# Regrouping the attention of a four-layer transformer kernel: two bursts per period in place of three

## The chip, the cores and the metric

The kernel runs on one core of a Trainium2 chip. The metric is the device time of one execution in microseconds (us). The engines of the core run side by side: TensorE (PE in the profile, its weight loads are PEld), VectorE (DVE), ScalarE (ACT), GpSimd (POOL), and SyncE (SP), which here only issues transfers. TensorE writes its results to PSUM, which this kernel uses as eight banks of 128 x 512 numbers in f32; ACT and DVE read a bank and so make it free again.

## The reference

The input `x` has 2048 rows of 640. Four layers are added to it in turn, A, B, A, B, each on a layer norm of what is there. Both kinds have 32 heads of width 20.

```python
# A: linear attention
pq, pk = phi(q), phi(k)
kv  = einsum("bhsd,bhse->bhde", pk, v);  z = einsum("bhsd->bhd", pk)
o   = (pq @ kv) / (pq @ z + 1e-6)                 # then @ wo
# B: four segments of 512 rows, with a memory over the segments before
logits = q_s @ k_s.T * scale + causal_mask        # 512 x 512 for each head
a_dot  = softmax(logits) @ v_s
a_mem  = (phi(q_s) @ M) / (phi(q_s) @ z + 1e-6)
o      = g * a_mem + (1 - g) * a_dot              # then @ wo
M, z   = M + phi(k_s).T @ v_s, z + sum(phi(k_s))
```

The change concerns `a_dot` alone.

## The kernel before

Two streams of instructions are made and merged. The **dense** stream makes projections, memories, transposes and output products of all layers; its large parts are the lines 388 (a product of 15 matmuls of 320 columns) and 374 (15 matmuls of 512 columns). The **attention** stream makes `a_dot` of the two B layers. `Kernel.run` takes from the stream whose planned cost so far is smaller. TensorE's order is exactly the order in which the code is written (`MANUAL = ("PE",)`). The other engines' instructions are ordered by a scheduler.

Attention goes by groups of four heads: eight groups in a segment, four segments, two B layers, so 64 groups. Of a group, the heads are named by `p` and `par` (0 or 1 each). Keys and queries of `par` 0 lie in rows 0 to 63 and those of `par` 1 in rows 64 to 127, and the matmuls of two `par` run beside each other on the two halves of TensorE. Blocks of 128 rows of a segment are counted by `i` (queries) and `j` (keys); only blocks with j <= i are computed, so a row of blocks has 512, 384, 256 or 128 columns. A group needs these steps:

- `max`, `row_max`, line 999 on TensorE: scores with a query block stationary, five parts (`MAXES`) of two PSUM banks each; DVE takes the maximum of each row in line 1006. `split` (lines 1015 and 1016) and `rows` (a transpose on TensorE in line 1024, a copy on ACT in line 1026, two transfers on SP) put the negative maxima as extra rows into the query stack `qs`.
- `exp`, `scores`, line 1041 on TensorE: scores with a key block stationary, with the maxima subtracted, five parts (`EXPS`) of two banks. ACT takes the exponential of each bank (line 1045, result `pe`), and POOL sets the blocks on the diagonal to zero above it (line 1052, a select). Parts 0 and 1 hold the key block j = 0; part 2 the blocks j = 1 and 3 of `p` = 0; part 3 the same of `p` = 1; part 4 the block j = 2 of all four heads.
- `sum`, `weigh`, line 1068 on TensorE: the four heads' exponentials times the values of block j, on four column groups at once, in f32, into one bank `pv`. So `sum` 1 and `sum` 3 need `exp` 2 and 3, and `sum` 2 needs `exp` 4.
- `copy` (ACT, line 1074) empties `pv`; `out` (line 1081, four transposes on TensorE, then DVE lines 1084 and 1091 and an addition on POOL or DVE) normalizes.

The order of these steps is written out by hand in `STRETCHES`. Each entry names the step, its part, and how many periods back the group is that it works on (0 the newest group, 2 the oldest). One pass over all stretches is a period. All that one stretch issues follows on TensorE without dense work in between (a burst). After a stretch the attention stream yields `SLOT`, the planned cost of the dense work that is let in behind it, in ns.

PSUM banks come from one pool with eight buffers, shared by both streams:

```python
def bank(self):
    return self.ps.tile([P, 512], F32, tag="ps", name="ps", bufs=8)
```

Of the kernel before, what the change touches and what calls it, by code (L numbers as in the profile page):

```python
# [39 lines left out]
VW = H * E1 + 11  # L40
HB = H // 2
COL = 1 / 2.4
SLOT = 2420.0
R_SECOND, R_PROJ, R_MID, R_END = 2.2, 1.0, 1.2, 0.85


# [5 lines left out]
EXPS += [[((0, a, 2, 0), (1, a, 2, 256)) for a in range(2)]]  # L52


STRETCHES = [[("exp", 4, 2), ("max", 0, 0), ("max", 1, 0), ("sum", 0, 2), ("rows", 0, 1), ("sum", 1, 2), ("sum", 3, 2),
              ("sum", 2, 2), ("copy", 0, 2), ("max", 2, 0)],
             [("out", 0, 2), ("exp", 0, 1), ("exp", 1, 1), ("max", 3, 0)],
             [("exp", 2, 1), ("exp", 3, 1), ("max", 4, 0), ("split", 0, 0), ("load", 0, 0)]]


def constants():
# [69 lines left out]
class Kernel:  # L131
# [965 lines left out]
    def attention(self, segs):  # L1097
# [3 lines left out]
        while n < NSEG * NG or prev or old:  # L1101
# [7 lines left out]
            n += 1  # L1109
            for stretch in STRETCHES:  # L1110
                for op, k, back in stretch:
# [18 lines left out]
                    elif op == "out":  # L1130
                        if not G["st"].get("remembered"):
                            yield lambda: G["st"].get("remembered")
                        self.normalize(G)
                yield SLOT
            old, prev = prev, new
# [192 lines left out]
```

## Time and profile before

| what | value |
|---|---|
| median of 3 runs | 1765.23 us (1764.43 to 1766.04) |
| the profiled execution | 1769.35 us, its span 1767.6 us |
| TensorE busy | 1683.3 us, 95% of the span |
| DVE, ACT, POOL busy | 1195.1, 971.2 and 517.4 us |
| mean granted TensorE clock | 0.992 |

The profile is of one execution. A busy TensorE counts each matmul from its start to a modelled end, and matmuls overlap by about 0.17 us, so short stalls are partly hidden in the busy time; distances from start to start tell more. Attention of the first B layer lies between about 350 and 953 us of the span, that of the second between about 1214 and 1743 us.

### The profile page before, as it was taken

The page shows a single profiled execution, that of the slowest core. Times are in us where ns is not written, and L with a number is a line of the kernel's source. Part 1 is how long each engine was busy: PE and PEld are TensorE (multiplying, and loading weights), DVE is VectorE, ACT ScalarE, POOL GpSimd, SP SyncE. Part 2 cuts the span into 40 slices and gives each one's busy share as a digit, 9 for nine tenths or more (in the row PEclk, how much of TensorE's full clock was granted, in tenths as well). Part 3 has the DMA queues.
Part 4 walks back from the last instruction along what each step waited for, and adds up shares of the span by engine and source line. Part 5 has one row for each costly group of instructions (what it writes and reads, how often), then busy time and mean ns, then how long its engine had stood idle before and what let it go on. Part 6 is the DMA issues. An engine that isn't in the chain of part 4 may idle for free.

```text
span 1767.6 us, 36360 instructions
## 1 busy us (share of the span) xinstructions
PE 1683.3 (95%) x13032; PEld 1050.2 (59%) x13032; DVE 1195.1 (68%) x3856; ACT 971.2 (55%) x1818; POOL 517.4 (29%) x982
## 2 busy tenths in 40 slices
PE   5989999999999999999989999999999999999998
PEld 4666667564565576456556777566546545644555
DVE  7554434487787677658864465846888877878773
ACT  5454443347656645567666453333675576666664
POOL 1533441012123312333342211221421432233452
PEclk9999999999999999999999999999999999999999
DMA  6432343422322322353211303433232323223432
GB/s 245 155 133 105 142 167 110 154 71 72 109 84 67 110 96 80 113 161 99 80 42 39 113 31 120 157 107 121 69 102 83 109 80 105 93 84 107 130 110 90
DMA packets 118333, 187.61 MB, mean 106 GB/s; under 512 B 13948, under 2 KB 79612, under 8 KB 115848
## 3 DMA queue, kind: packets, MB, share of 16 engines
q1 hardware_dynamic: 105896, 142.68, 25.5%
q0 software_dynamic: 3040, 21.63, 3.4%
q10 hardware_dynamic: 9216, 20.98, 3.1%
q8 instruction: 103, 1.69, 0.4%
q14 instruction: 78, 0.64, 0.1%
HBM read 106.05 MB, written 78.64 MB: 104 GB/s over the span
## 4 chain that ended last, share of the span: by engine, by line
PE 73%; DVE 12%; ACT 6%; issue 3%; DMA 3%; POOL 2%; SPq 0%; ACTq 0%; DVEq 0%; POOLq 0%
PE ps L388 31%; PE ps L374 15%; PE ps L1068 6%; DVE junk L1006 4%; PE ps L1041 3%; PE ps L313 3%; PE ps L999 3%; ACT pe L1045 3%; PE ps L557 3%; PE ps L443 3%; PE ps L884 1%; PE ps L1081 1%; PE ps L723 1%; DMA qs<-mt 1%; DVE st L331 1%
## 5 line engine op out<-in xcount | busy, mean ns | idle before, releaser
L1006 DVE CUSTOM_DVE_ANT_0 junk<-ps,maskw 128x512 bf16<-128x512 f32 (+3 forms) x1024 | 499.4, 488 | 94.3 <-PE ps L999 34.0
L1045 ACT ACTIVATE pe<-ps,lsc 128x512 f32<-128x512 f32 x640 | 394.7, 695 | 100.4 <-PE ps L1041 97.1
L1052 POOL TENSOR_SCALAR_AFFINE_SELECT pe<-pe 128x256 f32<-128x256 f32 (+1 forms) x640 | 229.6, 365 | 453.6 <-ACT pe L1045 449.3
L388 PEld LDWEIGHTS <-xT 128*128 128x128 f16 x2880 | 281.7, 99 | 115.7 <-issue 9.7
L388 PEld LDWEIGHTS <-oT 128*128 128x128 f16 x1920 | 186.5, 99 | 82.6 <-issue 7.5
L1068 PE MATMUL ps<-pe,v 128*32 128x512 f32 (+3 forms) x2048 | 161.5, 439 | 7.7 <-POOL pe L1052 3.4
L388 PE MATMUL ps<-w_Bo,oT 128*128 128x320 f16 x960 | 144.5, 304 | 2.3 <-ACT oT L317 1.2
L374 PE MATMUL ps<-xT,w_Bq 128*128 128x512 f16 x600 | 142.1, 383 | 1.7 <-ACT pe L1045 0.8
L388 PE MATMUL ps<-w_Bv,xT 128*128 128x320 f16 x960 | 140.7, 301 | 0.7 <-ACT v L421 0.7
L999 PE MATMUL ps<-ks,qs 60*128 60x384 f16 (+3 forms) x1024 | 128.8, 298 | 12.5 <-DVE mg L1006 3.6
L374 PE MATMUL ps<-xT,w_Bk 128*128 128x512 f16 x600 | 138.8, 379 | 1.0 <-DVE mg L1006 0.5
L388 PE MATMUL ps<-w_Ak,xT 128*128 128x320 f16 x960 | 137.3, 300 | 0.6 <-ACT r L402 0.5
L1041 PE MATMUL ps<-qs,ks 62*128 62x512 f16 (+3 forms) x1024 | 107.4, 301 | 5.4 <-DMA qs<-mt 3.7
L414 POOL TENSOR_SCALAR e<-e 128x320 f32<-128x320 f32 (+1 forms) x52 | 82.1, 1578 | 88.7 <-ACT e L410 85.7
L849 DVE SCALAR_TENSOR_TENSOR nat<-ps,nat 128x512 f16<-128x512 f32 x80 | 54.9, 687 | 77.9 <-ACT nat L848 71.2
L1068 PEld LDWEIGHTS ps<-pe,v 128*32 128x32 f32 x2048 | 63.7, 110 | 65.3 <-issue 43.8
L848 ACT ACTIVATE nat<-ps 128x512 f16<-128x512 f32 x80 | 48.1, 601 | 94.8 <-PE ps L374 70.9
L999 PEld LDWEIGHTS <-qs 60*128 60x128 f16 x1024 | 51.1, 94 | 82.5 <-issue 55.1
L374 PEld LDWEIGHTS <-w_Bq 128*128 128x128 f16 x600 | 57.1, 98 | 67.0 <-issue 9.8
L374 PEld LDWEIGHTS <-w_Bk 128*128 128x128 f16 x600 | 57.4, 98 | 65.2 <-issue 5.3
L336 POOL TENSOR_TENSOR rs<-rs,mhalf 128x1 f32<-128x1 f32 x48 | 27.0, 564 | 227.0 <-DVE rs L335 214.3
L421 ACT ACTIVATE v<-ps 128x320 f32<-128x320 f32 x96 | 41.7, 436 | 91.5 <-PE ps L388 90.2
(220 smaller groups left out, 2680.3 us busy)
## 6 DMA issues: line engine op xcount, KB each, us to landing
x<-xn ACTq DMA_DIRECT2D x48, 320.0 KB
qs<-qd SPq DMA_DIRECT2D x128, 120.0 KB
ks<-kd SPq DMA_DIRECT2D x128, 120.0 KB
xo<-x SPq DMA_DIRECT2D x48, 320.0 KB
pqi<-pqd SPq DMA_DIRECT2D x32, 320.0 KB
qd<-nat SPq DMA_DIRECT2D x40, 256.0 KB
kd<-nat SPq DMA_DIRECT2D x40, 256.0 KB
x<-in_A_x SPq DMA_DIRECT2D x16, 320.0 KB
```

The costliest lines, as they stand in the source:

```text
L313: nc.tensor.transpose(pt[:, (c - c0) * P:(c - c0 + 1) * P], src[:, c * P:(c + 1) * P], self.ident)
L374: nc.tensor.matmul(p, w[:, c, a, t * P:(t + 1) * P], xT[:, c, b, :], start=k == 0, stop=k == 3 * C - 1)
L388: nc.tensor.matmul(p, xT[:, c, a, i * P:(i + 1) * P], w[:, c, b, n * HN:(n + 1) * HN], start=k == 0, stop=k == 3 * C - 1)
L414: nc.gpsimd.tensor_scalar(e, e, 1.0, eps, op0=OP.min, op1=OP.add)
L443: nc.tensor.matmul(nd[:, lo - k * cut:hi - k * cut], pq[t], mem[:, OFF[t] + lo - a:OFF[t] + hi - a], start=first, stop=True, skip_group_ch ...
L849: nc.vector.scalar_tensor_tensor(nat[:, 1], p, QK_SHIFT, nat[:, 0], op0=OP.mult, op1=OP.subtract)
L999: nc.tensor.matmul(bs[par][:, a:a + n], qs[r, p, i * P:(i + 1) * P], ks[r, p, :n], start=True, stop=True)
L1006: nc.vector.tensor_tensor_reduce(junk[:, :n], bs[par][:, a:a + n], self.maskw[:, SEG - n:], 1.0, NEG, OP.add, OP.max, G["mg"][:, par, p, i ...
L1041: nc.tensor.matmul(b[:, a:a + n], ks[r, p, j * P:(j + 1) * P], qs[r, p, j * P:], start=True, stop=True)
L1045: nc.scalar.activation(e, b, AF.Exp, scale=self.lsc)
L1052: nc.gpsimd.affine_select(d, d, pattern=pat, compare_op=OP.is_ge, fill=0.0, base=0, channel_multiplier=-1)
L1068: nc.tensor.matmul(G["pv"][32 * h4:32 * h4 + 32, j * P:], v[j][:, h * E1:h * E1 + 32], G.pop((p, par, j)), start=j == 0, stop=j == 2, skip ...
```

## The change

The three stretches become two, and `SLOT` grows by half, so that the planned dense work of a period (2 x 3630 against 3 x 2420 ns) stays the same.

```diff
-SLOT = 2420.0
+SLOT = 3630.0
...
-STRETCHES = [[("exp", 4, 2), ("max", 0, 0), ("max", 1, 0), ("sum", 0, 2), ("rows", 0, 1), ("sum", 1, 2), ("sum", 3, 2),
-              ("sum", 2, 2), ("copy", 0, 2), ("max", 2, 0)],
-             [("out", 0, 2), ("exp", 0, 1), ("exp", 1, 1), ("max", 3, 0)],
-             [("exp", 2, 1), ("exp", 3, 1), ("max", 4, 0), ("split", 0, 0), ("load", 0, 0)]]
+STRETCHES = [[("exp", 3, 2), ("max", 0, 0), ("exp", 4, 2), ("max", 1, 0), ("sum", 0, 2), ("rows", 0, 1), ("sum", 1, 2),
+              ("sum", 3, 2), ("sum", 2, 2), ("copy", 0, 2), ("max", 2, 0)],
+             [("out", 0, 2), ("exp", 0, 1), ("exp", 1, 1), ("max", 3, 0), ("exp", 2, 1), ("max", 4, 0), ("split", 0, 0),
+              ("load", 0, 0)]]
```

`exp` 3 moves from the old third burst to the head of the next first burst, with `max` 0 between it and `exp` 4. `exp` 2, `max` 4, `split` and `load` move to the end of the second burst. No instruction of a group is added or taken away.

On ACT, in a period of the first B layer, the rows before are these: two exponentials (L1045) of the first burst, the copies L1026 and L1074 at its end, and then the eight exponentials of the second and third burst.

```order
L421 ACTIVATE v_82<-ps 128x16x20
L1045 ACTIVATE pe<-ps,lsc 128x512 x2
L1026 ACTIVATE mt<-pm 32x128
L1074 ACTIVATE oTf<-ps,cg 128x512
L465 ACTIVATE xn<-ps,ioB 128x320
L1045 ACTIVATE pe<-ps,lsc 128x512 x8
L317 ACTIVATE oT<-ps 128x2x128
```

The same place of the changed program, on ACT again:

```order
L421 ACTIVATE v_82<-ps 128x16x20
L1045 ACTIVATE pe<-ps,lsc 128x512 x4
L1026 ACTIVATE mt<-pm 32x128
L1074 ACTIVATE oTf<-ps,cg 128x512
L465 ACTIVATE xn<-ps,ioB 128x320
L1045 ACTIVATE pe<-ps,lsc 128x512 x6
L317 ACTIVATE oT<-ps 128x2x128
```

Four exponentials now stand in the first burst instead of two, and six in the second instead of four and four in two bursts. They keep their place ahead of the dense copies (L317, L465).

On TensorE, the first burst of the same period runs into its weighing (L1068) like this before, with a transpose of the maxima (L1024) between its parts; the values `v_83` to `v_86` are those of the blocks 0 to 3:

```order
L999 MATMUL ps<-ks_2758,qs 128x128
L1068 MATMUL ps<-pe,v_83 32x512 x4
L1024 LDWEIGHTS m_6698
L1024 MATMUL pm<-ident_70,m_6698 32x128
L1068 MATMUL ps<-pe,v_84 32x384 x4
L1068 MATMUL ps<-pe,v_86 32x128 x4
L1068 MATMUL ps<-pe,v_85 32x256 x4
```

The head of the changed first burst on TensorE, at the seam between `exp` 3, `max` 0 and `exp` 4 (`ks_2759` are the keys of the oldest group, `ks_2758` those of the newest):

```order
L1041 LDWEIGHTS ks_2759
L1041 MATMUL ps<-qs,ks_2759 128x128
L999 LDWEIGHTS qs
L999 MATMUL ps<-ks_2758,qs 128x512
...
L1041 MATMUL ps<-qs,ks_2759 128x256
```

The order within the weighing is unchanged, block 2 (`v_85`, which needs `exp` 4) last; ahead of it `exp` 4 now stands behind `exp` 3 and `max` 0 instead of at the head of the burst.

## The prediction

> **What bounds the kernel now.** I read the page's busy times first, then the two attention stretches by window, then one period on the timeline, engine by engine.
>
> ```profile
> PE 1683.3 (95%) x13032; PEld 1050.2 (59%) x13032; DVE 1195.1 (68%) x3856; ACT 971.2 (55%) x1818; POOL 517.4 (29%) x982
> PE 73%; DVE 12%; ACT 6%; issue 3%; DMA 3%; POOL 2%; SPq 0%; ACTq 0%; DVEq 0%; POOLq 0%
> 350.00:953.00 603.00, 578.67 (x4757) 349.08 (x4754) 450.97 (x1621) 369.40 (x687) 177.69 (x404) 0.99 0.29 88
> 1214.00:1745.00 531.00, 506.12 (x4199) 289.74 (x4197) 410.00 (x1475) 332.45 (x609) 181.65 (x395) 0.99 0.30 96
> ```
>
> The first line is the busy time by engine, the second the chain that ended last, the others the stretches with attention (length, then PE, PEld, DVE, ACT, POOL, the granted clock). TensorE is 96% busy there, DVE 75 to 77%, ACT 61 to 63%. Its order is fixed, so whatever holds a matmul holds all behind it. The time is TensorE's own work, which the change leaves as it is, plus its waits and what it loses between kinds of matmul. One undisturbed period on TensorE (start, length, shape, count):
>
> ```profile
> 538.25 0.84 PE L388 MATMUL ps<-w_Bv,xT 128*128 128x320 f16 x5
> 539.03 0.40 PE L1041 MATMUL ps<-qs,ks 62*128 62x256 f16 x4
> 539.26 0.60 PE L999 MATMUL ps<-ks,qs 60*128 60x512 f16 x6
> 539.79 1.06 PE L1068 MATMUL ps<-pe,v 128*32 128x512 f32 x8
> 541.54 0.64 PE L1068 MATMUL ps<-pe,v 128*32 128x256 f32 x8
> 542.12 0.39 PE L999 MATMUL ps<-ks,qs 60*128 60x512 f16 x2
> 542.44 0.55 PE L313 MATMUL ps<-ident,otok 128*128 128x128 f32 x3
> 542.82 2.20 PE L388 MATMUL ps<-w_Bv,xT 128*128 128x320 f16 x15
> 544.86 0.60 PE L1081 MATMUL ps<-ident,oTf 128*128 128x128 f32 x4
> 545.39 0.61 PE L1041 MATMUL ps<-qs,ks 62*128 62x512 f16 x4
> 545.84 0.38 PE L999 MATMUL ps<-ks,qs 60*128 60x384 f16 x4
> 546.15 0.44 PE L313 MATMUL ps<-ident,otok 128*128 128x128 f32 x2
> 546.42 2.20 PE L388 MATMUL ps<-w_Bv,xT 128*128 128x320 f16 x15
> 548.56 0.61 PE L1041 MATMUL ps<-qs,ks 62*128 62x384 f16 x8
> 549.00 0.45 PE L999 MATMUL ps<-ks,qs 60*128 60x256 f16 x4
> 549.39 0.33 PE L313 MATMUL ps<-ident,otok 128*128 128x128 f32 x1
> ```
>
> From start to start, burst 1 takes 3.41 us (539.03 to 542.44), burst 2 1.29 (544.86 to 546.15), burst 3 0.83 (548.56 to 549.39). The weighing of block 2, `sum` 2, starts 2.51 us into burst 1, and 0.90 us remain from there. What feeds TensorE in that period, on ACT, POOL and DVE:
>
> ```profile
> 539.51 1.26 ACT L1045 ACTIVATE pe<-ps,lsc 128x512 f32<-128x512 f32 x2
> 540.85 0.41 POOL L1052 TENSOR_SCALAR_AFFINE_SELECT pe<-pe 128x256 f32<-128x256 f32 x1 [0.17 <-ACT pe L1045]
> 545.88 2.42 ACT L1045 ACTIVATE pe<-ps,lsc 128x512 f32<-128x512 f32 x4 [0.38 <-PE ps L1041]
> 545.79 0.49 DVE L1091 TENSOR_TENSOR tmp<-ps,rc 128x320 f32<-128x320 f32 x1
> ```
>
> Two exponentials end 1.26 us after the first starts, four 2.42, so each further one costs 0.58. The second select of `exp` 4 ends at 541.26, only 0.28 us before `sum` 2 starts at 541.54. That slack is what the change spends.
>
> **The removed burst.** Fifteen matmuls of line 388 take 2.04 us up to the transposes (542.82 to 544.86) but 2.14 up to a score matmul (546.42 to 548.56): entering a burst costs 0.10. Leaving costs as much: the last pair of 512 columns takes 0.32 (542.12 to 542.44), against 0.225 inside a burst (half of 545.39 to 545.84). One burst fewer saves 0.2 us a period, over some 60 periods 12 us. The page "TensorEngine Tiling (Array Packing)" of the Trainium skill, section "Key Properties", says that changing the tiling mode drains the TensorE; by that rule alone the change is a gain, and the rows agree on the sign, at 0.1 us a change.
>
> **`exp` 3 at the head of burst 1.** Its 8 weight loads and 8 matmuls move and cost what they did: half of 548.56 to 549.00, 0.22. Its two exponentials now stand ahead of those of `exp` 4 on ACT. The first starts 0.48 us into the burst as before; four end at 0.48 + 2.42 = 2.90; the last select ends 0.49 later as now (541.26 against 540.77), at 3.39, and TensorE follows at about 3.44. Its own work would bring it to `sum` 2 at 2.51 + 0.22 = 2.73. So `sum` 2 waits 0.7 us, and burst 1 takes 3.44 + 0.90 = 4.34, 0.93 more than now. `sum` 1 is hardly held: the selects of `exp` 3 are done at 2.23, and its second half starts around then. Queued behind `sum` 2 are `max` 2, all dense work, and ACT's copy of `pv`. Bounds: if ACT starts at once, at 0.3, it is 0.75; with a copy of 0.5 in front, 1.4.
>
> **The merged burst.** It writes 11 banks (1 `out`, 4 for `exp` 0 and 1, 2 `max` 3, 2 `exp` 2, 2 `max` 4), where burst 2 wrote 7 and the pool has 8. In the built program the ninth bank is mostly `out`'s, which DVE frees at 546.28, 1.42 us into the burst; the last `max` 4 bank is the second exponential's, and the first dense bank behind it the third's (30 of 62 periods) or that of `max` 3 (15). The third exponential ends at 545.88 + 2.42 - 0.58 = 547.72, so dense work resumes 2.9 us after `out` begins, whatever TensorE could do. Now bursts 2 and 3 and an entry cost 1.29 + 0.83 + 0.10 = 2.22: 0.7 more. The next dense bank is often the fourth exponential's, 0.58 later; where the first dense piece is a transpose of 0.3 to 0.4 us, in about two periods of five, that adds 0.2, so 0.1 on average. The trace has a natural experiment, a period in which bursts 2 and 3 nearly met:
>
> ```profile
> 1651.81 0.61 PE L1041 MATMUL ps<-qs,ks 62*128 62x512 f16 x4
> 1653.61 0.37 PE L1041 MATMUL ps<-qs,ks 62*128 62x384 f16 x2 [0.20 <-ACT pe L1045]
> 1654.19 0.38 PE L1041 MATMUL ps<-qs,ks 62*128 62x384 f16 x2 [0.20 <-ACT pe L1045]
> 1654.77 0.40 PE L999 MATMUL ps<-ks,qs 60*128 60x256 f16 x4 [0.20 <-ACT pe L1045]
> 1655.62 3.87 PE L388 MATMUL ps<-w_Bo,oT 128*128 128x320 f16 x15 [0.46 <-ACT pe L1045]
> 1652.30:1655.70 3.40, 2.34 (x21) 1.01 (x18) 2.44 (x10) 3.40 (x7) 2.57 (x7) 1.00 0.02 5
> 1655.80:1659.20 3.40, 3.40 (x15) 1.91 (x13) 2.08 (x10) 1.50 (x3) 1.52 (x4) 0.50 0.01 2
> ```
>
> TensorE goes step by step at ACT's 0.58 us, each step released by an exponential; from 1651.81 to the dense matmul it took 3.81 us with eight exponentials. The changed burst has six.
>
> **The clock.** The last two rows above are windows: after one with 2.34 us busy of 3.40 the clock was 0.50 for the next, and 15 matmuls took 3.87 us instead of 2.20, a price of 1.67. The changed burst has about 1.2 us of waits, somewhat less than this window; I take that 8 of 60 periods trip it, 13 us (bounds 0 and 20 periods, 33 us). The Trainium skill, "TensorE: Matmul & The Clock Gate", section "Why this matters for your kernels", puts the fall at idle gaps of over about 3 us; by that rule no wait here reaches it and the sum is 13 us lower. The row disagrees (no wait in that window is near 3 us), and I go by the row.
>
> **Moved at no cost.** `exp` 2, `max` 4, `split` and `load` only come earlier: DVE gets the same maxima, SP the four transfers of `load` 1.2 us of dense work sooner before their use. Without that cover a late transfer holds TensorE, for 2.89 us where it happened (next row); with more cover that can only shrink. Dense copies on ACT stand behind six exponentials instead of four, up to 1.16 us later; 3.6 us of dense work between bursts cover it, and if not, part of it comes on top (0 to 0.3 a period, taken as 0).
>
> ```profile
> 721.17 1.26 PE L1041 MATMUL ps<-qs,ks 62*128 62x512 f16 x4 [2.89 <-DMA qs<-mt]
> 384.60 0.39 PE L1041 MATMUL ps<-qs,ks 62*128 62x256 f16 x4
> 1713.80 0.40 PE L1041 MATMUL ps<-qs,ks 62*128 62x256 f16 x4
> ```
>
> **Waits of before that go.** The last two rows are the first and the last of the 60 whole bursts of kind 1; from first to last the three kinds average 3.88, 1.65 and 1.02 us, that is 0.47 + 0.36 + 0.19 = 1.02 us a period over the undisturbed one, 61 us in all. Much of it is DVE and ACT being late, and those engines now get 10% more time per period; a late start of ACT, though, moves the new chains by as much. I let two thirds go: 41 us (bounds 0 and 61).
>
> **The sum.** Per period 0.93 + 0.7 + 0.1 = 1.73 (entry and exit are inside the two differences), times 60 = 104; less 41, plus 13: 76 us. The profiled execution took 1769.35 us (span 1767.6), so 1845 for it; it lay 4 us above the median of the runs, so 1841.
>
> **Rivals.** (1) Faster. The waits are hidden and the lost burst counts: 12 us and most of the 33 us of waits in bursts 2 and 3 go, 1720 to 1753. It decides if `exp` 4 is selected by 2.73 us into burst 1, that is if four exponentials take 1.7 us; they take 2.42 in the row, and the merged burst needs 11 banks of 8. Chance 0.05. (2) Mild: all 61 us of old waits go, the clock never falls, ACT starts early in burst 1 (0.75 in place of 0.93) and the second dense wait (0.1) never comes: 60 x 1.45 - 61 = 26, 1791 or less; 0.07, nearly no change 0.02 of it. DVE's and ACT's room to catch up speaks for it, their unchanged pace within a burst against. (3) The clock falls in every second period: 30 x 1.67 = 50 instead of 13, and few old waits go: 1892 or more; 0.08. The window above speaks for it; the changed burst's two fewer exponentials against. The forecast, 1791 to 1892, has 0.80: its low end is where the mild case begins, its high end no old wait gone and 13 periods throttled (1765 + 104 + 22 = 1891).
>
> About 0.2% is what a measurement of this kernel can tell from no change. Faster 0.05, same 0.02, slower 0.93.
>
> **What would show it.** Burst 1 of 4.2 to 4.7 us with TensorE waiting for POOL's select (line 1052) ahead of the last line 1068; dense work about 2.9 us or more after line 1081, waiting for ACT's line 1045; some 60 waits of each, where TensorE's waits for these are few now. I am wrong if burst 1 stays below 4.0, if the merged burst ends near 1.8, or if dense stalls grew instead.

## The result, and the profile after

| | before | after |
|---|---|---|
| median of the runs on one chip | 1765.26 us | 1870.88 us (1868.47 to 1872.99) |
| profiled execution, its span | 1769.35, 1767.6 us | 1869.62, 1867.8 us |
| mean granted clock | 0.992 | 0.991 |
| stretches with attention | 604 + 529 us | 657 + 577 us |

The ratio is 1.0607 (95% interval 1.0596 to 1.0618): slower by 105.6 us, where 76 were forecast, inside the range. The spans of the two profiled executions differ by 100.2 us, since the one before lay 4 us above the median of its runs; all of that lies in the attention stretches (+53 and +48 us from their first to their last attention matmul). The busy line, the chain and the two stretches of the changed kernel, in the form shown of before:

```profile
PE 1742.6 (93%) x13032; PEld 1079.2 (58%) x13032; DVE 1203.1 (64%) x3856; ACT 970.7 (52%) x1818; POOL 520.2 (28%) x982
PE 59%; ACT 9%; DVE 6%; issue 2%; POOL 2%; DMA 1%; ACTq 0%; SPq 0%; DVEq 0%; POOLq 0%
349.00:1006.00 657.00, 612.01 (x4763) 365.31 (x4764) 458.63 (x1622) 370.56 (x688) 178.38 (x404) 0.99 0.26 81
1267.00:1844.00 577.00, 530.80 (x4194) 301.97 (x4193) 409.56 (x1473) 330.34 (x607) 182.96 (x394) 0.99 0.28 89
```

The chain that ended last now runs over ACT for 9% in place of 6 and over TensorE for 59% in place of 73. No engine got more instructions: ACT is busy 56 to 57% of these stretches in place of 61 to 63, DVE 70 to 71 in place of 75 to 77. TensorE's busy time grew by 59 us although it runs the same 13032 matmuls, whose lengths sum to the same (4281 us before, 4283 after): what grew is the time in which at least one of them is open, since a matmul ahead of a wait overlaps the next one less. So the distances from start to start count, here of one undisturbed period, both bursts and the dense work behind each:

```profile
559.96 0.40 PE L1041 MATMUL ps<-qs,ks 62*128 62x384 f16 x4
561.28 1.07 PE L1068 MATMUL ps<-pe,v 128*32 128x512 f32 x8 [0.27 <-ACT pe L1045]
562.17 1.86 PE L1068 MATMUL ps<-pe,v 128*32 128x384 f32 x24
562.94 0.41 POOL L1052 TENSOR_SCALAR_AFFINE_SELECT pe<-pe 128x256 f32<-128x256 f32 x1 [0.17 <-ACT pe L1045]
564.28 0.55 PE L313 MATMUL ps<-ident,otok 128*128 128x128 f32 x3
566.70 0.60 PE L1081 MATMUL ps<-ident,oTf 128*128 128x128 f32 x4
567.72 3.58 ACT L1045 ACTIVATE pe<-ps,lsc 128x512 f32<-128x512 f32 x6 [0.38 <-PE ps L1041]
569.04 0.38 PE L999 MATMUL ps<-ks,qs 60*128 60x256 f16 x3 [0.31 <-ACT pe L1045]
569.62 0.44 PE L313 MATMUL ps<-ident,otok 128*128 128x128 f32 x2 [0.20 <-ACT pe L1045]
```

Burst 1 lasts 4.32 us (559.96 to 564.28). Its last select ends at 563.35, 3.39 us into it, and 0.93 later dense work resumes. The merged burst lasts 2.92 us (566.70 to 569.62). The six exponentials run through, 0.57 to 0.58 us from one start to the next; the second ends at 568.98 and lets the last maxima go on at 569.04, the third lets dense work go on at 569.62. The next rows give TensorE's idle time ahead of all instructions of a group (the first number behind the second bar, in us) and what ended most of it. The first pair is before, the second after; in each, the first row is the scores for the maxima and the second the weight loads of the weighing:

```profile
L999 PE MATMUL ps<-ks,qs 60*128 60x384 f16 (+3 forms) x1024 | 128.8, 298 | 12.5 <-DVE mg L1006 3.6 <-ACT pe L1045 3.1 <-DVE oT L318 2.2
L1068 PEld LDWEIGHTS ps<-pe,v 128*32 128x32 f32 x2048 | 63.7, 110 | 65.3 <-issue 43.8 <-POOL pe L1052 17.1 <-POOL xn L466 2.6
```

```profile
L999 PE MATMUL ps<-ks,qs 60*128 60x512 f16 (+3 forms) x1024 | 152.5, 298 | 35.5 <-ACT pe L1045 23.5 <-DVE mg L1006 6.4 <-DVE tmp L1091 1.6
L1068 PEld LDWEIGHTS ps<-pe,v 128*32 128x32 f32 x2048 | 76.7, 109 | 97.5 <-POOL pe L1052 47.2 <-issue 41.6 <-POOL xs L506 0.5
```

The waits for banks that ACT frees rose from 3.1 to 23.5 us in line 999, and the weight loads of the weighing waited 47.2 us for POOL's select in place of 17.1.

All bursts, from the first attention matmul to the next dense one, read from the starts in the trace:

| us | before: least, mean, sum | after: least, mean, sum |
|---|---|---|
| burst 1, 60 of them | 3.41, 3.88, 232.7 | 4.32, 4.97, 298.1 |
| burst 2 (60), burst 3 (62); after: merged (60) | 1.29, 1.67, 100.0; 0.76, 1.12, 69.7 | 2.85, 3.31, 198.3 |
| incomplete ones at the ends of a layer | 26.4 | 34.2 |
| all | 428.8 in 202 bursts | 530.6 in 136 |

That is +101.8 us. The 66 bursts fewer save 0.1 us each at their entry (6.6); dense matmuls at half clock lose 15.8 us in place of 9.1 (+6.7); other dense stalls (what a dense matmul takes to the next start beyond the usual of its shape) went from 49.5 to 48.6 (-0.9). Together +101, and the span grew by 100.2.

### The profile page after: what moved, and what is told of

Read it like the earlier page. It is cut to its first block, busy times and chain, and to the rows that moved or that the text cites. A ratio compares the mean times of both kernels' runs of the same rounds, so it can differ in the third digit from the quotient of the medians.

```text
span 1867.8 us, 36362 instructions
## 1 busy us (share of the span) xinstructions
PE 1742.6 (93%) x13032; PEld 1079.2 (58%) x13032; DVE 1203.1 (64%) x3856; ACT 970.7 (52%) x1818; POOL 520.2 (28%) x982
## 3 DMA queue, kind: packets, MB, share of 16 engines
q8 instruction: 103, 1.69, 0.4%
## 4 chain that ended last, share of the span: by engine, by line
PE 59%; ACT 9%; DVE 6%; issue 2%; POOL 2%; DMA 1%; ACTq 0%; SPq 0%; DVEq 0%; POOLq 0%
PE ps L388 23%; PE ps L374 12%; PE ps L1068 8%; ACT pe L1045 6%; PE ps L1041 3%; PE ps L557 3%; PE ps L443 3%; PE ps L313 2%; PE ps L999 2%; DVE junk L1006 1%; PE ps L884 1%; PE ps L1081 1%; POOL pe L1052 1%; ACT r L412 1%; PE ps L876 1%
## 5 line engine op out<-in xcount | busy, mean ns | idle before, releaser
L1045 ACT ACTIVATE pe<-ps,lsc 128x512 f32<-128x512 f32 x640 | 388.0, 696 | 85.2 <-PE ps L1041 82.1
L1068 PE MATMUL ps<-pe,v 128*32 128x512 f32 (+3 forms) x2048 | 186.9, 438 | 22.7 <-POOL pe L1052 12.2
L999 PE MATMUL ps<-ks,qs 60*128 60x512 f16 (+3 forms) x1024 | 152.5, 298 | 35.5 <-ACT pe L1045 23.5
L1041 PE MATMUL ps<-qs,ks 62*128 62x384 f16 (+3 forms) x1024 | 133.2, 299 | 12.0 <-ACT pe L1045 7.6
L1068 PEld LDWEIGHTS ps<-pe,v 128*32 128x32 f32 x2048 | 76.7, 109 | 97.5 <-POOL pe L1052 47.2
L999 PEld LDWEIGHTS <-qs 60*128 60x128 f16 x1024 | 55.7, 93 | 122.7 <-issue 93.9
L466 POOL TENSOR_TENSOR xn<-xn,xo 128x320 f32<-128x320 f32 x56 | 48.7, 871 | 172.6 <-ACT xn L465 172.6
```

Of the source, the lines that this page charges most:

```text
L999: nc.tensor.matmul(bs[par][:, a:a + n], qs[r, p, i * P:(i + 1) * P], ks[r, p, :n], start=True, stop=True)
L1041: nc.tensor.matmul(b[:, a:a + n], ks[r, p, j * P:(j + 1) * P], qs[r, p, j * P:], start=True, stop=True)
L1045: nc.scalar.activation(e, b, AF.Exp, scale=self.lsc)
L1068: nc.tensor.matmul(G["pv"][32 * h4:32 * h4 + 32, j * P:], v[j][:, h * E1:h * E1 + 32], G.pop((p, par, j)), start=j == 0, stop=j == 2, skip ...
```

## The experiments

The theory: in a burst, TensorE outruns ACT. What it writes or weighs beyond some point goes at ACT's 0.58 us for an exponential and then POOL's select, and more exponentials in one burst than eight PSUM banks and the order of the weighing can hide are paid in full. The main rivals were: the burst structure itself (fewer, longer bursts and longer dense pieces) costs; the one part of the change is harmless and the other does it all; or POOL's select alone does it.

Mean lengths of the bursts of every kernel, to be looked up below (us; "four" has its last two bursts in the third and fourth place, and a few of its bursts that ran together are in the sum alone). Ratios are taken to runs of the kernel before beside each experiment, with medians of 1763.72 to 1764.74 us.

| kernel | median | 1 | 2 or merged | 3 | 4 | all bursts |
|---|---|---|---|---|---|---|
| before | 1765.26 | 3.88 | 1.67 | 1.12 | | 428.8 |
| after | 1870.88 | 4.97 | 3.31 | | | 530.6 |
| three, `exp` 3 moved | 1798.81 | 5.05 | 1.51 | 0.66 | | 463.6 |
| two, `exp` 3 not moved | 1857.07 | 3.70 | 4.06 | | | 500.3 |
| two, half the exponentials | 1748.54 | 4.15 | 2.37 | | | 419.7 |
| three, half the exponentials | 1739.55 | 3.76 | 1.64 | 0.97 | | 407.8 |
| two, no select | 1842.55 | 4.44 | 3.37 | | | 500.5 |
| three, no select | 1756.17 | 3.69 | 1.72 | 1.13 | | 419.7 |
| three, `exp` 4 in burst 3 | 1793.82 | 3.31 | 1.69 | 1.93 | | 443.7 |
| four, `max` 4 last | 1817.44 | 4.35 | 1.85 | 0.69 | 0.36 | 466.4 |
| four, no `exp` in burst 1 | 1824.81 | 3.97 | 1.87 | 0.70 | 0.84 | 470.3 |
| four, `exp` 3 last | 1788.44 | 3.91 | 1.88 | 0.72 | 0.35 | 440.9 |
| three, maxima one burst later | 1833.13 | 4.20 | 1.54 | 1.95 | | 491.8 |
| three, `rows` behind `sum` 1 | 1767.82 | 3.84 | 1.71 | 1.14 | | 430.2 |

### The two parts alone

Three bursts as before, with `exp` 3 at the head of the first:

```diff
-STRETCHES = [[("exp", 4, 2), ("max", 0, 0), ("max", 1, 0), ...
+STRETCHES = [[("exp", 3, 2), ("max", 0, 0), ("exp", 4, 2), ("max", 1, 0), ...
...
-             [("exp", 2, 1), ("exp", 3, 1), ("max", 4, 0), ("split", 0, 0), ("load", 0, 0)]]
+             [("exp", 2, 1), ("max", 4, 0), ("split", 0, 0), ("load", 0, 0)]]
```

> Three bursts as before with SLOT 2420, and only exp 3 moved from the third burst to the head of the first, as in the change. Theory A (two separate holds: in burst 1 the four exponentials and the select ahead of sum 2; in the merged burst the banks that ACT frees one by one): burst 1 averages about 4.9 us as in the changed kernel (4.97 against 3.88 before, 60 bursts, +65 us), burst 3 loses its 0.22 us of matmuls and a part of its waits (-13 to -25 us): 1800 to 1820. Rival B (only the merging costs, exp 3 just fills time at the head of burst 1): 1755 to 1775, burst 1 at 3.6.

Measured: 1798.81 us, ratio 1.0195 (1.0179 to 1.021), just under the theory's figure and far from the rival's. Burst 1 is that of the changed kernel (least 4.32 us, sum 303.2, +70.5 over before); the shorter third burst gives back 27.4 and the second 9.4. So this part costs 34 us without any merging.

Two bursts, `exp` 3 left in the second of them:

```diff
-SLOT = 2420.0
+SLOT = 3630.0
...
-             [("out", 0, 2), ("exp", 0, 1), ("exp", 1, 1), ("max", 3, 0)],
-             [("exp", 2, 1), ("exp", 3, 1), ("max", 4, 0), ("split", 0, 0), ("load", 0, 0)]]
+             [("out", 0, 2), ("exp", 0, 1), ("exp", 1, 1), ("max", 3, 0), ("exp", 2, 1), ("exp", 3, 1), ("max", 4, 0),
+              ("split", 0, 0), ("load", 0, 0)]]
```

> Two bursts with SLOT 3630, but exp 3 stays behind exp 2 in the second burst, and the first burst is that of before. Theory A: burst 1 is back at 3.4 at the least and 3.9 on average; the merged burst writes 13 banks and dense work waits for the fifth exponential: 1.70 + 4 x 0.58 + 0.05 = about 4.1 us from line 1081 to the dense matmul, against 2.2 for bursts 2 and 3 undisturbed and 2.9 on average: +70 to +110 us, and more windows at half clock (10 to 30 us): 1845 to 1900. Rival B' (the merging is cheap and the hold in burst 1 is all): 1750 to 1775.

Measured: 1857.07 us, ratio 1.052 (1.0501 to 1.0538). Burst 1 is back at its 3.41. The merged burst is at least 3.49 us, less than the 4.1 expected: dense work goes on behind the fourth exponential, not the fifth. One of the shortest bursts, on TensorE and ACT (line numbers are two lower in this kernel):

```profile
411.11 0.60 PE L1079 MATMUL ps<-ident,oTf 128*128 128x128 f32 x4
412.12 4.73 ACT L1043 ACTIVATE pe<-ps,lsc 128x512 f32<-128x512 f32 x8 [0.38 <-PE ps L1039]
414.60 1.24 PE L372 MATMUL ps<-xT,w_Bq 128*128 128x512 f16 x5 [0.18 <-ACT pe L1043]
```

Four exponentials take 2.42 us and end at 414.54, 0.06 before dense work. Dense work follows the fourth within 0.12 us in 25 of the 60 merged bursts and a later one in 8; in the others no exponential ends so near. So for these bursts the expectation counted one exponential too many; which other reader freed a bank in its place the rows do not name. The merging alone is worth most of the loss (92 us), and with it `exp` 3 in burst 1 makes it only 14 us worse, since it takes two exponentials out of the merged burst (4.06 to 3.31). The parts do not add: 34 and 92 against 106 together.

### The pace of ACT: half of the exponentials left out

The changed kernel without the exponentials and selects of the heads of `par` 1; the weighing reads a constant tile for them, and `pe` has nine buffers in place of ten to make room for it. The control is the kernel before with the same cut.

```diff
+        self.flat = self.bp.tile([P, 512], F32, name="flat")
+        nc.gpsimd.memset(self.flat, 0.5)
...
+        if todo[0][1] == 1:
+            for p, par, j, a in todo:
+                G[p, par, j] = self.flat[:, a:a + SEG - j * P]
+            return cost
```

> The changed kernel with half of the exponentials left out: of each pair of score banks only that of par 0 is read by ACT and selected by POOL; the weighing of par 1 reads a constant tile instead. TensorE's and DVE's work stay. Theory A (ACT's pace of 0.58 us a bank makes both holds): two exponentials are over 1.26 + 0.5 + 0.5 = 2.3 us into burst 1, ahead of sum 2 at 2.73, so burst 1 is 3.64 at its least; dense work resumes 1.7 to 2.1 us after line 1081. 1700 to 1750, and within 15 us of the three-burst kernel with the same left out, rather below it, since one entry and exit of a burst (0.2 us) is saved 60 times. Rival C (DVE's maxima or the change between kinds of matmul make the loss): the distance to the three-burst kernel stays at 60 us or more.

> The control of the kernel with half of the exponentials left out: the same left out of the kernel before, in three bursts. Theory A: most of the 61 us of waits in its bursts go too, since ACT is late in few of them: 1710 to 1745. Rival C: 1755 to 1765, as before, since ACT is not what its bursts wait for.

Measured: 1748.54 us for two bursts (ratio 0.9914, 0.9899 to 0.9929) and 1739.55 for three (0.9856, 0.9841 to 0.9871). The least burst 1 is 3.63 us, as worked out, the least merged burst 1.80, near TensorE's own work. TensorE's matmuls, the number of bursts and the dense pieces are those of the whole kernels, but two bursts are now only 9 us behind three, where they were 106 behind. So with half of the exponentials and selects some 97 of the 106 us are gone. That two bursts stayed behind at all was not expected, since 66 entries fewer are worth 7 us. Their bursts are still 12 us longer in sum. The 0.22 us by which the least burst 1 is longer (3.63 against 3.41) do not count here: they are `exp` 3's own matmuls, which left the third burst. Beyond its least length burst 1 waits 10 us more (31 against 21), incomplete bursts at the ends of a layer make 4 more, and dense stalls outside of bursts are 50.4 us against 43.4; why these grew is open.

### The select alone

POOL's select left out of the changed kernel and of the kernel before (the diagonal blocks are not masked then):

```diff
-        nc.gpsimd.affine_select(d, d, pattern=pat, compare_op=OP.is_ge, fill=0.0, base=0,
-                                channel_multiplier=-1)
```

> The changed kernel without POOL's select: the causal mask on the diagonal blocks is left out. Theory A (burst 1 is held by four exponentials and then a select before sum 2): sum 2 can start 0.49 us sooner, right behind the last exponential at 2.90 + 0.05, so burst 1 is 3.85 at its least in place of 4.32, and about 4.5 on average in place of 4.97 (-28 us); the merged burst stays as it is at 2.85 at the least and 3.3 on average: 1835 to 1850. Rival D (burst 1 is held by the bank that the first weighing needs, not by the select): 1862 to 1873, burst 1 still 4.3 at the least.

> The kernel before with POOL's select (line 1052) left out, so the mask on the diagonal is missing from the result; the control of the same cut in the two-burst kernel, which made that 28 us faster. If the two bursts put the select on the path (theory A), it lies off the path here: TensorE waits 2.8 us for it in all 60 first bursts, and few other waits hang on it; the time falls by 0 to 12 us, to 1752 to 1764, first bursts keep their minimum of 3.41 us. Rival: the select costs the same in both kernels (POOL work in the way of all engines), then 1733 to 1742.

Measured: 1842.55 us for two bursts (ratio 1.0439, 1.0423 to 1.0455), 28 less than with the select; 1756.17 for three (0.996, 0.9947 to 0.9972), 7.6 less than before in the runs beside it (1763.72). In two bursts burst 1 falls to at least 3.82 and on average 4.44 us, the merged burst does not change (3.31 and 3.37). So the select is worth some 20 of the 106 us, on the side of burst 1. The other 77 of the 97 above would be ACT's exponentials if the two simply add; no run leaves out the exponentials and keeps the selects, so this split is worked out and not shown.

### Where else could the exponentials go

If the second burst of the changed kernel is too full, fewer in the first or more and smaller bursts might be faster than before. Three bursts with `exp` 4 moved from burst 1 into burst 3:

```diff
-STRETCHES = [[("exp", 4, 2), ("max", 0, 0), ("max", 1, 0), ...
+STRETCHES = [[("max", 0, 0), ("max", 1, 0), ...
...
-             [("exp", 2, 1), ("exp", 3, 1), ("max", 4, 0), ("split", 0, 0), ("load", 0, 0)]]
+             [("exp", 2, 1), ("exp", 3, 1), ("exp", 4, 1), ("max", 4, 0), ("split", 0, 0), ("load", 0, 0)]]
```

> Three bursts, with exp 4 moved from the head of burst 1 into the third burst ahead of max 4, so that nothing in burst 1 waits for ACT. Theory A: burst 1 is 3.19 at the least and 3.4 to 3.6 on average (-17 to -28 us), the third burst writes 8 banks with six exponentials, and the dense matmul behind it waits for the first exponential (1.2 us at the least, 1.5 to 1.8 on average, +23 to +40 us): 1760 to 1785. Rival F (waiting for ACT in burst 1 is all there is to gain, banks don't bind with 8): 1735 to 1750.

Measured: 1793.82 us, ratio 1.0167 (1.0147 to 1.0186), above what was expected. Burst 1 does lose nearly all its stalls (mean 3.31 over a least of 3.19 us, 34 us less in sum). Burst 3 now writes eight banks and gains 50 (mean 1.93 over a least of 1.17, where it was 1.12 over 0.76); dense stalls grow by 9 and half-clock dense work by 5. In and right behind burst 3, TensorE's idle time that an exponential ends rises from 4 to 20 us: dense work goes on at the end of the first exponential in 24 of these bursts, of a later one in 19. The pool has eight banks, so a burst of eight that waits for exponentials finds some of them still held; that the dense work ahead holds them is an inference.

Four bursts, in two ways (`SLOT` 1815, so that a period has the same dense work):

```diff
-             [("exp", 2, 1), ("exp", 3, 1), ("max", 4, 0), ("split", 0, 0), ("load", 0, 0)]]
+             [("exp", 2, 1), ("exp", 3, 1)],
+             [("max", 4, 0), ("split", 0, 0), ("load", 0, 0)]]
```

> The kernel before with its third burst cut in two (exp 2 and 3; max 4, split and load), SLOT 1815, so four bursts per period. It measures by itself what one more entry and exit of a burst costs. Theory A (0.1 us each way): +0.2 us in 62 periods, +12 us, less what waits in the third burst go as ACT gets a pause there (up to 15 us): 1760 to 1778. Rival E (changes between kinds of matmul cost several tenths, so fewer bursts ought to be a large gain): 1790 or more.

The other has `exp` 4 taken out of burst 1 as well and put at the head of the fourth:

```diff
+             [("exp", 4, 1), ("max", 4, 0), ("split", 0, 0), ("load", 0, 0)]]
```

> Four bursts, SLOT 1815: burst 1 without exponentials, then exp 0 and 1 with out and max 3, then exp 2 and 3 alone, then exp 4 with max 4. No burst needs more than 7 banks and none waits for its own exponentials. Theory A: burst 1 as in the kernel with exp 4 early (3.19 at the least, 3.5 on average, -23 us), the two small bursts 0.55 and 0.55 at the least and 0.75 each on average with one more entry (0.75 + 0.75 + 0.1 against 1.12, +29 us), waits in burst 2 shrink a little (-5 us): 1755 to 1770. Rival F: 1735 to 1750.

Both expectations failed, by 39 and 55 us over their upper ends: 1817.44 us (ratio 1.03, 1.0285 to 1.0316) and 1824.81 (1.0342, 1.0317 to 1.0366). The first time lies in the range of rival E, but not for its reason: bursts 3 and 4 of that kernel sum to 65 us against 70 before, and outside of bursts its span grew by 11.6 us in all, so 54 more entries cost 0.2 us each at the most. Bursts 1 and 2 got longer, burst 1 at the transpose of the maxima. Before, the first four-burst kernel, the second:

```profile
L1024 PE MATMUL pm<-ident,m 128*32 128x128 f16 x64 | 14.1, 221 | 5.2 <-DVE m L1016 5.0 <-DVE oT L318 0.2
```

```profile
L1024 PE MATMUL pm<-ident,m 128*32 128x128 f16 x64 | 14.5, 227 | 12.5 <-DVE m L1016 12.1 <-DVE oT L318 0.2 <-ACT pe L1045 0.2
```

```profile
L1024 PE MATMUL pm<-ident,m 128*32 128x128 f16 x64 | 14.4, 226 | 21.8 <-DVE m L1016 21.5 <-DVE oT L318 0.2
```

The maxima are what is loaded as weights there, and the loads wait longer than the matmuls (before, then the first four-burst kernel; 49.2 us for DVE in the second):

```profile
L1024 PEld LDWEIGHTS <-m 128*32 128x32 f16 x64 | 6.1, 96 | 28.0 <-DVE m L1016 14.2 <-issue 11.6 <-DVE mg L1006 1.1
L1024 PEld LDWEIGHTS <-m 128*32 128x32 f16 x64 | 6.1, 95 | 45.5 <-DVE m L1016 36.3 <-issue 8.6 <-DVE mg L1006 0.5
```

A new theory: between `max` 4 and `rows` stood one piece of dense work of 2.42 us of planned cost, now one of 1.8, and DVE's last maxima come too late for the transpose. To tell this from "a fourth burst costs", one kernel keeps four bursts and gives DVE more distance, another keeps three bursts and the dense pieces and gives DVE less to spare:

```diff
+             [("exp", 2, 1), ("max", 4, 0), ("split", 0, 0), ("load", 0, 0)],
+             [("exp", 3, 1)]]
```

> Four bursts again, but the last cut the other way round: max 4, split and load stay with exp 2 in the third burst, exp 3 alone is the fourth, so that 3.63 us of dense work lie between max 4 and rows (1.8 in the two kernels with four bursts before this, 2.42 in the kernel before). If their loss was DVE's maxima coming late for the transpose L1024, the first burst comes back to a mean near 3.9 us (4.35 there) and the wait of L1024 for DVE to 5 us or less (10.8 there): 28 us less than 1817, so 1775 to 1795; what stays is the second burst's wait for max 2, which also has only 1.8 us of dense work behind it. Rival: a fourth burst, or shorter pieces of dense work, cost by themselves: 1808 to 1825 again.

```diff
-             [("out", 0, 2), ("exp", 0, 1), ("exp", 1, 1), ("max", 3, 0)],
-             [("exp", 2, 1), ("exp", 3, 1), ("max", 4, 0), ("split", 0, 0), ("load", 0, 0)]]
+             [("out", 0, 2), ("exp", 0, 1), ("exp", 1, 1), ("max", 2, 0)],
+             [("exp", 2, 1), ("exp", 3, 1), ("max", 3, 0), ("max", 4, 0), ("split", 0, 0), ("load", 0, 0)]]
```

> Three bursts and the same dense pieces as the kernel before, but the maxima one burst later: max 2 in the second burst, max 3 and max 4 both in the third. Number of bursts, exponentials and their places stay. If DVE's distance from the last maxima to rows is what made the kernels with four bursts slow, this one is slower too: two banks more for DVE in the last 2.42 us before rows, so L1024 waits for DVE in most periods by up to about 0.5 us, a first burst of 3.9 less 0.33 for max 2 plus 0.3 to 0.5, and 1775 to 1800 in all. Rival: DVE has room in three bursts, only the fourth burst was at fault: 1758 to 1770.

Measured: 1788.44 us with more distance (ratio 1.0142, 1.0128 to 1.0156), 29 less than the first four-burst kernel, and 1833.13 with less (1.0401, 1.0385 to 1.0417). The transpose in each (line numbers of the first are one higher):

```profile
L1025 PE MATMUL pm<-ident,m 128*32 128x128 f16 x64 | 14.0, 219 | 1.8 <-DVE oT L319 1.2 <-ACT v L422 0.5
```

```profile
L1024 PE MATMUL pm<-ident,m 128*32 128x128 f16 x64 | 14.6, 228 | 29.4 <-DVE m L1016 29.0
```

With 3.63 us of planned dense work in between, the wait of these matmuls for the maxima is gone from their row; with two more banks to read in the old 2.42 it is 29.0 us. So the distance of DVE makes 29 of the 54 us that the first four-burst kernel had lost, not the number of bursts. Two things went otherwise than expected. With the wait gone, four bursts still are 25 us behind before: burst 2 waits for the banks of `max` 2 (mean 1.88 us in place of 1.67, about 12 us in sum), 56 entries at 0.1 us would make some 6, and the rest is not accounted for. And the kernel with the late maxima is 33 us above its range: its third burst writes eight banks, as in the kernel with `exp` 4 there, and takes 51 us more than before, 28 of them in its least length (1.22 against 0.76) and 23 in waits beyond it.

The last kernel only moves `rows` behind `sum` 1:

```diff
-... ("sum", 0, 2), ("rows", 0, 1), ("sum", 1, 2), ("sum", 3, 2),
+... ("sum", 0, 2), ("sum", 1, 2), ("rows", 0, 1), ("sum", 3, 2),
...
```

> The kernel before with one step moved: rows (L1024) behind sum 1 instead of ahead of it, so that DVE has 0.5 us more for the last maxima. If the 5.0 us that L1024 waits for DVE in first bursts are a start of delays that then spread (they are 28 us over the minimum in all), the time falls by 5 to 15 us, to 1750 to 1760. Rival 1: the delays come from elsewhere and only move, 1762 to 1768. Rival 2: the transfers of the maxima start 0.5 us later and hold the second burst (qs from mt, 3.7 us now) more often: 1770 to 1785.

Measured: 1767.82 us, ratio 1.002 (1.001 to 1.0031). The wait of the transpose falls from 5.0 to 3.3 us, and what is won in burst 1 (2.4 us) is lost in burst 2 (2.8), where the wait for the transfer of `qs` rises from 3.7 to 5.6. The delays only move, the first rival; the time itself is 4 us above that of the runs beside it. No version that computes everything beat the kernel before.

## Why the prediction came out as it did

The way and the mechanism were right: both bursts are held as forecast. The size was 30 us low, and one term of the sum makes it: the waits of before, most of which were to go and did not.

**The removed burst: right, and as small as it was put.** The sum of the terms above closes on the span with 0.1 us an entry. The Trainium skill, page "TensorEngine Tiling (Array Packing)", section "Key Properties", has a change of the tiling mode drain TensorE. The trace agrees on the sign, at about 7 us for 66 entries. In the two-burst kernel with half the exponentials even these did not show in the time.

**Burst 1: right.** 4.34 us forecast, 4.32 the least; the last select ends 3.39 us into it, as worked out to the hundredth. The end of the last select decides when block 2 is weighed in 55 of the 60 bursts (about a dozen before). One wait was not named: the bank of `sum` 0 is the ninth of the burst, that of the first exponential, so the weighing starts at 1.32 us where it started at 0.76 (539.03 to 539.79 in the row of before). In the undisturbed burst the last select is later still, and the wait costs nothing.

**The merged burst: right in its least, small in its usual length.** 2.92 us forecast; 22 of 60 lie at 2.85 to 2.94. In 14 more it is 3.1 to 3.3, in 13 it is 3.4 to 3.6, and 11 are longer. For such a further step of an exponential I had put 0.1 us on average; the mean lies 0.39 over 2.92.

**The old waits: this step failed.** Two thirds, 41 of 61 us, were to go, above all because DVE and ACT get more time per period. The 61 was itself low: over all 62 of them, third bursts average 1.12 us and not 1.02. Taken over the least lengths, the waits were 73 us before (0.47 x 60 in burst 1, 0.38 x 60 in burst 2, 0.36 x 62 in burst 3) and are 66 after (0.65 and 0.45, times 60): 7 went. The least lengths themselves rose by 4.32 + 2.85 - 3.41 - 1.29 - 0.76 - 0.10 = 1.61 us a period, 97 us where 104 were forecast. In bursts 2 and 3 18 of 45 us went. In burst 1 the waits even grew, from 28 to 39 us, and the trace shows to what. On ACT, POOL and TensorE in the burst that starts at 449.68, which took 5.78 us:

```profile
450.28 1.26 ACT L1045 ACTIVATE pe<-ps,lsc 128x512 f32<-128x512 f32 x2
451.42 0.70 ACT L410 ACTIVATE e<-ps,inv_Bq 128x512 f32<-128x512 f32 x1
451.99 0.71 ACT L412 ACTIVATE r<-ps,inv_Bq 128x512 f32<-128x512 f32 x1
452.56 1.29 ACT L1045 ACTIVATE pe<-ps,lsc 128x512 f32<-128x512 f32 x2
```

```profile
453.34 1.18 POOL L1052 TENSOR_SCALAR_AFFINE_SELECT pe<-pe 128x256 f32<-128x256 f32 x2 [1.33 <-ACT pe L1045]
```

```profile
449.68 0.40 PE L1041 MATMUL ps<-qs,ks 62*128 62x384 f16 x4
452.57 1.05 PE L1068 MATMUL ps<-pe,v 128*32 128x384 f32 x16
454.22 0.99 PE L1068 MATMUL ps<-pe,v 128*32 128x256 f32 x8 [0.60 <-POOL pe L1052]
455.46 0.44 PE L876 MATMUL ps<-ident,pkT 128*128 128x128 f32 x2
```

Two activations of the dense stream (lines 410 and 412) stand between the second and the third exponential and push the chain by 1.14 us. In 14 of the 60 first bursts ACT has dense work inside the chain (in 5 before, when the chain had two), and the four exponentials then take 3.43 us on average, against 2.45 in the others. Summed over the 60 bursts, ACT's later start (over 0.48 us) makes 10 us, its longer chain (over 2.42) 16 and later selects (over 0.49) 10, together 36 of the 39 us. Over the 60 bursts, length and end of the last select go together with a correlation of 0.98 and a slope of 0.97 us per us. Before, the same three delays (the chain over 1.26) sum to 29 us, but block 2 had 0.28 us of slack, which took 8 of them, and it followed the select directly in about a dozen bursts only. The prediction had this mechanism ("a late start of ACT, though, moves the new chains by as much") and left a third of the old waits for it; in burst 1 it takes nearly all. That DVE and ACT have 10% more time a period shows nowhere in burst 1: in the 14 bursts ACT was late by its order and not by its load. Whether it helped the merged burst is not shown.

**The clock: right in kind, about half in size.** 13 us were forecast, 6.7 measured, in 11 windows of 3.41 us at half clock in the whole trace in place of 8. In the kernel with two bursts and `exp` 3 not moved there are 25 windows of half clock, and dense work in them loses 28 us more than before, at a mean clock of 0.977. That is the way of the third rival, at about half of its 50 us, and in another kernel than the changed one.

**Not counted: the ends of the layers.** The incomplete periods, which the 60 do not hold, grew by 8 us. So the sum runs: 97 in place of 104, -7 in place of -41, +7 in place of +13, +8 for the ends, and -3 for two third bursts more than 60 and the dense stalls: +102, against 100 by the spans and 76 by the forecast. The old waits make 34 us of the miss; that the other errors (-7, -6, +8 and -3) nearly cancel was luck. The rivals fell as their terms said: neither the faster (bursts of 3.4 and 1.8) nor the mild case (least lengths with no wait left) is seen, and the time stayed below 1892.

## What to carry to other kernels

These are rules of thumb from this one kernel. Before pieces of work are put together on one engine, count the banks they write and the rows of the engine that empties them: what goes beyond the pool, less the banks that other work still holds, runs at the emptying engine's pace, however idle that engine is on average. Waits on a path with slack are no reserve: once the new path hangs on the late engine without slack, every delay of that engine counts one to one, so carry old delays over in full unless a row shows that their cause goes. And a result that has to return to the fixed order (here the maxima) needs its distance in work of the engine that waits; cutting bursts smaller took that distance away here.

## What was not expected of the hardware

The clock fell without any long idle time. Three windows of the kernel with two bursts and `exp` 3 not moved, and what followed each (length, then PE, PEld, DVE, ACT, POOL, the granted clock):

```profile
612.24:615.65 3.41, 2.37 (x17) 1.25 (x17) 2.50 (x11) 3.41 (x7) 2.90 (x8) 1.00 0.01 2
615.65:619.06 3.41, 3.30 (x9) 1.13 (x8) 2.13 (x12) 1.40 (x3) 0.83 (x3) 0.50 0.25 96
629.30:632.71 3.41, 2.27 (x18) 1.33 (x14) 2.54 (x9) 3.41 (x7) 2.17 (x6) 1.00 0.53 162
632.71:636.12 3.41, 3.41 (x15) 2.07 (x14) 1.81 (x10) 1.16 (x3) 1.02 (x3) 0.50 0.00 0
970.62:974.03 3.41, 1.59 (x12) 1.25 (x13) 2.19 (x9) 2.53 (x4) 1.48 (x2) 1.00 0.26 99
974.03:977.45 3.42, 3.05 (x26) 1.54 (x24) 3.21 (x11) 3.42 (x7) 3.00 (x3) 1.00 0.00 0
```

In the first two, TensorE was busy for 2.37 and 2.27 us of 3.41, in pieces, with no idle time of more than 0.7 us, and the next 3.41 us ran at half clock. The Trainium skill, page "TensorE: Matmul & The Clock Gate", section "Why this matters for your kernels", puts the fall at idle gaps of over about 3 us; these rows disagree, and the measurement decides. Yet the busy time that the profile shows does not decide it either: the third window was busy for 1.59 us only, with one wait of 1.86 us, and the clock stayed at 1.00. What the clock goes by stays open here.
